# Matmuls without readers at two places of PE's queue in an attention, expert and dense-layer kernel

## The chip, the cores and the metric

The kernel runs on one core of a Trainium2 chip. The metric is device microseconds of one execution; a figure is the median of several. One further execution was taken by the hardware profiler, and all rows and durations below are from that one.

## What is computed

```python
attn_out = _attn_ref(q, k, v, f)                    # 4 x 8 heads, 576 x 64, causal, with decay
x = attn_out.transpose(0, 2, 1, 3).reshape(2304, 512)
# experts: each of 2304 tokens goes to the expert with the largest logit
logits = xn @ en.T / tau
expert_idx = np.argmax(logits, axis=1)
for e in range(8):
    mask = expert_idx == e
    h = np.maximum(x[mask] @ w1[e], 0.0)            # 512 -> 1024
    out[mask] = gate_w[mask, None] * (h @ w2[e])    # 1024 -> 512
# dense layers
h = x @ w_in                                        # 512 -> 2048
g = np.maximum(h, 0.0) + np.log1p(np.exp(-np.abs(h)))
y = g @ w_out                                       # 2048 -> 512
```

## The kernel before

Every instruction stands in the order in which the code writes it; each engine (PE, DVE, ACT, POOL) and SP, which issues most DMAs, works through its own queue in that order and waits for counters that the others raise.

**Attention** goes over 16 pairs of heads. Its last steps (`finish2`, `pick`) give every token's expert as a one-hot `oh`.

**Routing** turns these into slots of 128 tokens. `ranks` counts, on PE, each token's place in its expert's list into the PSUM tile `rk`; `places` (line 653) reads it with some ten small DVE steps; `route` (line 674) works out which expert each slot has, builds the 0/1 matrices `pm` (line 709) and the right side `rhs` (lines 772 to 774), and sums 20 matmuls into `pid` (line 778). From `pid` DVE makes `gidx`, by which POOL gathers the token rows `xg` from HBM (line 899). All of this has PE idle but for `ranks` and `pid`. Both PSUM tiles come from the attention's pool `ps_s`, tag `s`, three buffers.

**Experts** run in 13 phases written out in `phases`: a big one has two slots, a small one has one. A phase transposes its gathered rows (`xprep`: PE line 915, ACT line 916, DVE line 917), multiplies by `w1` (lines 983, 946), takes the relu, and multiplies by `w2` (line 933). Weights arrive by `wsplit` for the next phase: SP loads a 512 KB `raw` (lines 863, 866, 878), ACT rounds it to `wh` (line 887), DVE subtracts to get `wl` (line 888), which frees the `raw` for SP's next load; there are four `raw` buffers. Results go to `yd` in HBM by POOL's scatter (line 924).

After the last phase there may be more small slots than the plan foresaw. `tails` handles these under nested `tc.If` (line 1031): every engine reads the number of slots (line 1073) and branches. With these inputs no tail is run. A branch that isn't taken still leads each engine over an instruction that first waits until the engine's own earlier work is done and then raises the engine's counter by what the skipped code would have raised it. Whoever waits for work that stands behind the branch, or for memory that the skipped code would have used, waits for this instruction too.

**Dense layers** (`ffn`). SP first loads four tiles `y` from `yd` (line 1161), then more `raw` weights (line 1101). DVE, ACT and POOL convert the weights (`conv.step`, lines 1115 to 1121); when 16 of the 32 pieces are done, DVE scales the four `y` (line 1171), PE transposes them (line 1175), and from there PE runs `h` (line 1188) and `o` (line 1230) in turn to the end, while the rest of the weights is converted beside them.

Of the kernel before, what the change touches and what calls it, by code (L numbers as in the profile page):

```python
# [9 lines left out]
F32 = mybir.dt.float32  # L10
# [33 lines left out]
def body(ctx, tc, q, k, v, f, emb, tau, w1, w2, win, wout, out):  # L44
# [27 lines left out]
    with ExitStack() as acc:  # L72
        ps_s = attention(tc, g, acc, q, k, v, f, emb, tau, w1)
        ring = ctx.enter_context(tc.tile_pool(name="ring", bufs=16, reuse_waits="tile"))

        def wtile(dt=F32R):
            return (ring.tile([128, 1024], dt, name="wh", tag="wh"), ring.tile([128, 1024], dt, name="wl", tag="wl"))

        g.wtile = wtile
        with ExitStack() as rtx:  # L80
            route(tc, g, rtx.enter_context(tc.tile_pool(name="r_p", bufs=1)), ps_s)
    experts(tc, g, w1, w2, win, wout, out)


# [4 lines left out]
def attention(tc, g, acc, q, k, v, f, emb, tau, w1):  # L89
    nc = tc.nc  # L90
    ident, xd, ncum, nrm = g.ident, g.xd, g.ncum, g.nrm
    with ExitStack() as ctx:
        cst = ctx.enter_context(tc.tile_pool(name="a_cst", bufs=1))
# [4 lines left out]
        ps_s = acc.enter_context(tc.tile_pool(name="a_ps", bufs=3, space=PSUM))  # L98
# [353 lines left out]
        oh = cst.tile([128, T, E], BF16, name="oh")  # L452
# [64 lines left out]
        for n in range(n_all + Lg + 1):  # L517
# [47 lines left out]
                    g.pre.append(r)  # L565
            if n == n_all:
                rk = rank_start(tc, g, ps_s, oh)
        places(tc, g, cst, rk, oh)
    return ps_s


# [62 lines left out]
def rank_start(tc, g, psp, oh):  # L634
    nc = tc.nc
    rk = psp.tile([128, T + 1, E], F32, name="rk", tag="s")
    nc.tensor.matmul(rk, g.onesb, g.e4096, start=True, stop=False)
    nc.tensor.matmul(rk[:, T], g.onesb, oh[:, 0], start=False, stop=False)
    nc.tensor.matmul(rk[:, 1:T], g.onesb, oh[:, 0:1].to_broadcast([128, T - 1, E]), start=False, stop=False)
    ranks(nc, g, rk, oh, 0, T - 5)  # L640
    return rk


def ranks(nc, g, rk, oh, t0, t1):
    nc.tensor.matmul(rk[:, t0:t1], g.trib, oh[:, t0:t1], start=False, stop=False)
    for t in range(max(t0, 1), t1):
        nc.tensor.matmul(rk[:, t + 1:T + 1], g.onesb, oh[:, t:t + 1].to_broadcast([128, T - t, E]), start=False,
                         stop=(t == T - 1))

def places(tc, g, p, rk, oh):
    V = tc.nc.vector
    ranks(tc.nc, g, rk, oh, T - 5, T)
    sel = p.tile([128, T, E], F32, name="sel")
    V.tensor_tensor(sel, rk[:, 0:T], oh, op=ALU.mult)
    q = p.tile([128, T], F32, name="q")
    V.tensor_reduce(q, sel, op=ALU.add, axis=AX.X)
    g.n = g.const.tile([128, 3, E], I32, name="n")
    V.tensor_scalar(g.n[:, 0], rk[:, T], 0.0, None, op0=ALU.max)  # L660
    qi = p.tile([128, T], I32, name="qi")
    V.tensor_tensor(qi, q, g.inv.rearrange("p b r -> p (b r)"), op=ALU.add)
    V.tensor_scalar(g.n[:, 1], g.n[:, 0], 7, None, op0=ALU.logical_shift_right)
    li = p.tile([128, T], I32, name="li")
    V.tensor_scalar(li, qi, 127, None, op0=ALU.bitwise_and)
    V.tensor_scalar(g.n[:, 2], g.n[:, 1], 0x7FFFFFFE, None, op0=ALU.bitwise_and)
    g.lo = g.const.tile([128, T], F32, name="lo")
    V.tensor_copy(g.lo, li)
    g.code = g.const.tile([128, T, 1], I32, name="code")
    V.tensor_scalar(g.code[:, :, 0], qi, 7, None, op0=ALU.logical_shift_right)  # L670


def route(tc, g, p, psp):
    nc, lo, n, code = tc.nc, g.lo, g.n, g.code
# [4 lines left out]
    def tl(shape, nm, dt=F32):  # L679
        return p.tile(shape, dt, name=nm)  # L680
# [4 lines left out]
    start = tl([128, T, NSLOT], "start", BF16)  # L685
# [90 lines left out]
    pid = psp.tile([128, 3, NSLOT], F32, name="pid", tag="s")  # L776
    for t in range(T):
        nc.tensor.matmul(pid, pms[t], rhs[:, :, t], start=(t == 0), stop=(t == T - 1))
    pv = tl([128, 3, NSLOT], "pv")
    V.tensor_copy(pv[:, 1:3], pid[:, 1:3])  # L780
    V.scalar_tensor_tensor(g.gidx, pv[:, 1], 64.0, pv[:, 2], op0=ALU.mult, op1=ALU.add)
# [23 lines left out]
def gates(tc, g):  # L805
    nc = tc.nc
    V = nc.vector
    lt, nr, gs = g.lt, g.nr, g.gs
    nc.scalar.activation(nr[:, :, 0], g.nrm, ACTF.Sqrt)
    nc.scalar.preload_act_table_set(LN_EXP)  # L810
    V.tensor_scalar(nr, nr, 1e-6, None, op0=ALU.add)
    V.reciprocal(nr, nr)
    V.tensor_tensor(lt, lt, g.mx.to_broadcast([128, T, E]), op=ALU.subtract)
    V.tensor_tensor(lt, lt, nr.to_broadcast([128, T, E]), op=ALU.mult)
    nc.scalar.activation(lt, lt, ACTF.Exp)
    V.tensor_reduce(gs, lt, op=ALU.add, axis=AX.X)
    V.tensor_scalar(gs, gs, 1e-9, None, op0=ALU.add)
    V.reciprocal(gs, gs)
    for b in range(B):
        nc.gpsimd.dma_start(g.gd[b * S:b * S + 512, :].rearrange("(r p) o -> p (r o)", p=128), gs[:, 5 * b:5 * b + 4])  # L820
        nc.gpsimd.dma_start(g.gd[b * S + 512:b * S + S, :], gs[0:64, 5 * b + 4:5 * b + 5])
    nc.gpsimd.dma_start(g.gate, g.gd.rearrange("(t p) o -> p (t o)", p=128))


def experts(tc, g, w1, w2, win, wout, out):
    nc = tc.nc
# [10 lines left out]
    with ExitStack() as ctx:  # L837
        def pool(name, bufs, **kw):
            return ctx.enter_context(tc.tile_pool(name=name, bufs=bufs, reuse_waits="tile", **kw))
# [4 lines left out]
        ps_h = pool("e_ph", 3, space=PSUM)  # L844
# [219 lines left out]
        for ph in range(n_ph):  # L1064
            (big if phases[ph][0] == "b" else small)(ph)
            W.pop(ph)
            if ph == 0:
                gates(tc, g)
        while conv.done < PRE:
            conv.step(PRE - conv.done)  # L1070
        TW = [g.wtile() for _ in range(8)]
# [237 lines left out]
```

## Time and profile before

| | |
|---|---|
| median of 3 runs | 981.81 us (980.39 to 983.07) |
| the profiled execution | 986.43 us, of it 984.6 us from first to last instruction |
| mean granted clock of PE | 0.964 of full speed |
| PE busy | 904.0 us (92%) in 6340 matmuls |
| DVE, ACT, POOL busy | 647.8, 636.1, 362.0 us |
| routing, from the last `ranks` matmul to the first expert transpose | 252.13 to 267.33 us |
| from the last expert matmul to the first dense transpose | 546.66 to 564.97 us |

Times within the span count from its first instruction. The profiled execution is 4.6 us longer than the median of the unprofiled ones. A PE row's duration holds the fill and drain of the array, which overlap with the next one's; what a matmul costs in a stream is the distance between two starts.

### The profile page before, as it was taken

What the parts mean: (1) busy time and instruction counts of PE and PEld (TensorE: products, weight loads), DVE (VectorE), ACT (ScalarE), POOL (GpSimd) and SP (SyncE); (2) the same over time, 40 slices, a digit from 0 to 9 for tenths busy, and PEclk for the clock granted to TensorE, in tenths of its full rate; (3) what the DMA queues carried; (4) which work ended last, traced back from release to release, by engine and by line L of the source; (5) the groups of instructions that cost most, each with busy time, mean ns of one, the idle gap of its engine ahead of it and who ended that gap; (6) DMA issues with size and microseconds to landing.
All of it is one profiled execution on the core that took longest, in us unless ns stands there. A gap on an engine that the chain in (4) does not pass through costs nothing. (4 is left out here: it accounts for less than half of the span.)

```text
span 984.6 us, 17569 instructions
## 1 busy us (share of the span) xinstructions
PE 904.0 (92%) x6340; PEld 773.0 (79%) x6340; DVE 647.8 (66%) x1330; ACT 636.1 (65%) x1175; POOL 362.0 (37%) x438
## 2 busy tenths in 40 slices
PE   3999999999388899999998269999999999999998
PEld 2888888888276689889997258889988888998886
DVE  4888878887764668677674578885555545555454
ACT  4778877785463657666452257776767666677664
POOL 6655655551412321233222445652323222222221
PEclk9999999999589799999999789999999999999999
DMA  8766765840379889889874623301001001000001
GB/s 185 161 155 144 162 149 138 204 119 27 109 251 129 278 264 315 268 276 317 265 236 139 209 93 107 100 19 60 17 11 46 19 1 54 22 1 32 1 1 43
DMA packets 109852, 126.17 MB, mean 128 GB/s; under 512 B 62968, under 2 KB 72184, under 8 KB 109760
## 3 DMA queue, kind: packets, MB, share of 16 engines
q1 hardware_dynamic: 105952, 113.80, 41.7%
q0 software_dynamic: 3680, 11.03, 3.1%
q8 instruction: 52, 0.85, 0.4%
q14 instruction: 40, 0.33, 0.1%
q10 hardware_dynamic: 128, 0.16, 0.1%
HBM read 109.94 MB, written 15.03 MB: 127 GB/s over the span
## 5 line engine op out<-in xcount | busy, mean ns | idle before, releaser
L1218 DVE TENSOR_TENSOR gl<-e,gh 128x512 fp32r<-128x512 f32 (+1 forms) x80 | 97.6, 1220 | 152.7 <-ACT gh L1216 152.7
L1201 POOL TENSOR_TENSOR e<-u,e 128x512 f32<-128x512 f32 (+1 forms) x80 | 95.1, 1189 | 268.1 <-ACT u L1200 268.1
L888 DVE TENSOR_TENSOR wl<-raw,wh 128x1024 fp32r<-128x1024 f32 x100 | 122.8, 1239 | 72.4 <-ACT wh L887 69.9
L887 ACT ACTIVATE wh<-raw 128x1024 fp32r<-128x1024 f32 x100 | 104.7, 1057 | 50.4 <-DMA raw<-in_moe_w_dram 50.0
L1188 PE MATMUL h<-yth,wh 128*128 128x512 f32 (+1 forms) x320 | 120.0, 375 | 0.7 <-ACT yth L1176 0.7
L1188 PE MATMUL h<-ytl,wh 128*128 128x512 f32 (+1 forms) x320 | 118.5, 370 | 0.2 <-DVE ytl L1177 0.2
L1188 PE MATMUL h<-yth,wl 128*128 128x512 f32 (+1 forms) x320 | 118.4, 370 | 0.0
L1197 ACT ACTIVATE e<-h 128x512 f32<-128x512 f32 (+1 forms) x80 | 44.4, 555 | 107.2 <-PE h L1188 85.2
L1230 PE MATMUL o<-wl,gh 128*128 128x512 f32 x288 | 112.5, 391 | 0.0
L1230 PE MATMUL o<-wh,gh 128*128 128x512 f32 x288 | 112.4, 390 | 0.0
L1121 POOL TENSOR_TENSOR wl<-cv,wh 128x512 fp32r<-128x512 f32 x32 | 47.7, 1492 | 98.0 <-ACT wh L1120 79.0
L1230 PE MATMUL o<-wh,gl 128*128 128x512 f32 x288 | 80.8, 390 | 0.0
L300 ACT ACTIVATE pts<-pt 128x512 f16<-128x512 f32 (+3 forms) x128 | 58.7, 497 | 32.7 <-PE pt L313 17.6
L303 DVE SCALAR_TENSOR_TENSOR pts<-pt,pts 128x512 f16<-128x512 f32 (+3 forms) x128 | 69.7, 567 | 14.0 <-ACT pts L300 12.9
L946 PE MATMUL h<-xh,wh 128*128 128x256 f32 x256 | 73.2, 286 | 4.3 <-DVE hl L951 4.3
L946 PE MATMUL h<-xl,wh 128*128 128x256 f32 x256 | 73.0, 285 | 0.0
L946 PE MATMUL h<-xh,wl 128*128 128x256 f32 x256 | 73.0, 285 | 0.0
L933 PE MATMUL y<-wh,hh 128*128 128x512 f32 x168 | 69.2, 412 | 3.4 <-ACT hh L996 3.4
L1188 PEld LDWEIGHTS h<-yth,wh 128*128 128x128 f32 x320 | 60.6, 189 | 9.6 <-ACT yth L1176 1.1
L277 ACT ACTIVATE p<-sm,mx 128x512 f32<-128x512 f32 (+3 forms) x128 | 67.7, 558 | 0.0
L1188 PEld LDWEIGHTS h<-ytl,wh 128*128 128x128 f32 x320 | 60.6, 189 | 8.9 <-DVE ytl L1177 0.5
L933 PE MATMUL y<-wl,hh 128*128 128x512 f32 x168 | 67.1, 400 | 0.0
(273 smaller groups left out, 2424.7 us busy)
## 6 DMA issues: line engine op xcount, KB each, us to landing
raw<-in_moe_w_dram SPq DMA_DIRECT2D x104, 512.0 KB
cb<-ncum SPq DMA_DIRECT2D x32, 288.0 KB
raw<-in_moe_w_in_dram SPq DMA_DIRECT2D x16, 512.0 KB
raw<-in_moe_w_out_dram SPq DMA_DIRECT2D x16, 512.0 KB
cb<-ncum SPq DMA_DIRECT2D x32, 144.0 KB
out_dram<-ob SPq DMA_DIRECT2D x18, 256.0 KB
qt<-in_q_dram SPq DMA_DIRECT2D x32, 128.0 KB
kt<-in_k_dram SPq DMA_DIRECT2D x32, 128.0 KB
```

Source lines behind the costliest of these rows:

```text
L277: nc.scalar.activation(p[:, 0:n], s[:, 0:n], ACTF.Exp, scale=-1.0, bias=m)
L300: nc.scalar.activation(hi, ps, ACTF.Copy, scale=UP)
L303: nc.vector.scalar_tensor_tensor(lo, ps, UP, hi, op0=ALU.mult, op1=ALU.subtract)
L887: nc.scalar.activation(hi, r, ACTF.Copy)
L888: nc.vector.tensor_sub(lo, r, hi.bitcast(F32))
L933: nc.tensor.matmul(py[a], x[:, 128 * a:128 * a + 128], w[:, fb % 2], start=(fb == 0 and m == 0 and w is wh), stop=(fb == 7 and m == 1))
L946: nc.tensor.matmul(pl[:, a], w[:, fs], x[:, c], start=(c == 0 and m == 0), stop=(c == 3 and m == 2))
L1121: nc.gpsimd.tensor_sub(lo, a.bitcast(F32), hi.bitcast(F32))
L1188: nc.tensor.matmul(pl, w[:, fs], x[:, d], start=(d == 0 and m == 0), stop=(d == 3 and m == 2))
L1201: nc.gpsimd.tensor_sub(e, u, e)
L1218: nc.vector.tensor_sub(gl, d, gh.bitcast(F32))
L1230: nc.tensor.matmul(PO[c][a], x, w, start=(fb == 0 and m == 0 and w is wh), stop=(fb == FB - 1 and m == 1))
```

## The change

A matmul of `iof` (128 x 128, bf16, the numbers 0 to 127 in each row) with itself goes into a PSUM tile `idle` that nothing reads: 80 times behind the last of `ranks`, 40 times behind the last of `pid`, 220 times between the last expert phase and the branch of `tails`.

```diff
-        places(tc, g, cst, rk, oh)
+        places(tc, g, cst, rk, oh, ps_s)
...
+def busy(nc, g, psp, n):
+    t = psp.tile([128, 512], F32, name="idle", tag="s")
+    for _ in range(n):
+        nc.tensor.matmul(t[:, 0:128], g.iof, g.iof, start=True, stop=True)
...
-def places(tc, g, p, rk, oh):
+def places(tc, g, p, rk, oh, psp):
     V = tc.nc.vector
     ranks(tc.nc, g, rk, oh, T - 5, T)
+    busy(tc.nc, g, psp, 80)
     sel = p.tile([128, T, E], F32, name="sel")
...
         nc.tensor.matmul(pid, pms[t], rhs[:, :, t], start=(t == 0), stop=(t == T - 1))
+    busy(nc, g, psp, 40)
     pv = tl([128, 3, NSLOT], "pv")
...
             if ph == 0:
                 gates(tc, g)
+        t = ps_h.tile([128, 512], F32, name="idle", tag="h")
+        for _ in range(220):
+            nc.tensor.matmul(t[:, 0:128], g.iof, g.iof, start=True, stop=True)
         while conv.done < PRE:
             conv.step(PRE - conv.done)
```

The other engines' queues hold the same instructions in the same order as before. PE in the routing, with the change (`_49` ends the counters' names; `DMASW0` is the gather's; lines behind 655 are 8 or more higher than before):

```order
L647 MATMUL rk<-oh,onesb 128x8
L655 LDWEIGHTS iof
L655 MATMUL idle<-iof 128x128
...
L786 LDWEIGHTS pm [waits DVE_49,PE_49,Activation_49]
L786 MATMUL pid<-rhs,pm 128x75 [waits DVE_49]
...
L655 LDWEIGHTS iof
L655 MATMUL idle<-iof 128x128 [waits PE_49]
...
L924 MATMUL xt<-ident,xg 128x128 [waits DMASW0_49]
```

The 80 stand between `rk` and `pid`, the 40 between `pid` and the first transposes of gathered rows; each brings a load of its weights. They wait for no other engine.

PE at the branch, before:

```order
L933 MATMUL y<-wl,hh 128x512
L933 MATMUL y<-wh,hl 128x512
L1073 TENSOR_LOAD ids [waits Pool_49]
L1031 COMPARE_AND_BRANCH
...
L1031 UNCONDITIONAL_BRANCH [waits PE_49] x4
L1175 MATMUL yt<-ident,y_9160 128x128 [waits DVE_49,Activation_49]
```

and with the change:

```order
L942 MATMUL y<-wh,hl 128x512
L1080 LDWEIGHTS iof
L1080 MATMUL idle<-iof 128x128 [waits PE_49]
...
L1085 TENSOR_LOAD ids [waits Pool_49]
L1040 COMPARE_AND_BRANCH
...
L1040 UNCONDITIONAL_BRANCH [waits PE_49] x4
L1187 MATMUL yt<-ident,y_9503 128x128 [waits DVE_49,Activation_49]
```

The 220 stand ahead of the branch and of the instruction on the other path (shown with its wait for `PE_49`, PE's own counter) that PE must pass.

SP behind the branch, with the change (before, the same rows with the old line numbers):

```order
L1040 UNCONDITIONAL_BRANCH [waits SP_sequencer_49,DMAHW0_49,DMAHW1_49,DMAHW2_49,DMAHW3_49,DMAHW4_49,DMAHW5_49,DMAHW6_49,DMAHW7_49] x4
L1173 DMA y_9503<-yd 128x512 [waits DMASW4_49,DMASW3_49,DMASW5_49,DMASW2_49,DMASW6_49,DMASW1_49,DMASW7_49,DMASW0_49,DMAHW5_49,DVE_49,PE_49]
L1173 DMA y_9505<-yd 128x512 [waits DMAHW6_49,Activation_49]
L1173 DMA y_9507<-yd 128x512 [waits DMAHW7_49]
L1173 DMA y_9509<-yd 128x512 [waits DMAHW0_49]
L1113 DMA raw<-in_moe_w_in_dram 128x1024 [waits DMAHW1_49,DVE_49]
```

The first `y` load waits for PE's counter. In the built program of before it waits for 4592; PE's matmuls ahead of the branch bring the counter to 4364, and the instruction on the other path adds 240 once 4364 is reached. With the change the load waits for 4932; the matmuls, the 340 added ones among them, bring the counter to 4704, and the same instruction adds 240 once 4704 is reached.

## Rows read from the trace of the kernel before

**Rows 1.** The page's second part: busy tenths in 40 slices of 24.6 us.

```profile
PE   3999999999388899999998269999999999999998
PEclk9999999999589799999999789999999999999999
```

**Rows 2.** Timeline of PE, routing and first phase: start, duration, instructions, idle before and releaser.

```profile
251.84 0.29 PE L647 MATMUL rk<-oh,onesb 128*128 128x40 bf16 x5
261.28 1.43 PE L778 MATMUL pid<-rhs,pm 128*128 128x75 bf16 x20 [9.15 <-DVE rhs L774]
267.33 1.12 PE L915 MATMUL xt<-ident,xg 128*128 128x128 f32 x4 [4.62 <-DMA xg<-xd,gidx]
...
279.71 0.80 PE L933 MATMUL y<-wh,hh 128*128 128x512 f32 x1 [3.38 <-ACT hh L996]
```

**Rows 3.** Stretches of 4 us: PE, PEld, DVE, ACT, POOL busy, granted clock, DMA share, GB/s.

```profile
268.00:272.00 4.00, 3.90 (x11) 2.85 (x10) 2.96 (x4) 3.72 (x6) 3.17 (x4) 0.51 0.97 358
276.00:280.00 4.00, 0.62 (x3) 0.29 (x2) 0.79 (x1) 1.88 (x3) 0.00 (x0) 0.84 0.98 393
284.00:288.00 4.00, 4.00 (x20) 3.31 (x19) 2.65 (x4) 2.90 (x5) 0.00 (x0) 0.80 0.74 261
```

**Rows 4.** Timeline of PE from the last expert matmuls to the dense layers.

```profile
546.43 0.39 PE L933 MATMUL y<-wl,hh 128*128 128x512 f32 x1
546.66 0.39 PE L933 MATMUL y<-wh,hl 128*128 128x512 f32 x1
564.97 3.83 PE L1175 MATMUL yt<-ident,y 128*128 128x128 f32 x16 [17.93 <-DVE y L1171]
```

**Rows 5.** The chain that ended last, in order of time, 545 to 592 us.

```profile
553.82 0.33 SPq L1161
...
555.68 6.77 DMA raw<-in_moe_w_in_dram
```

**Rows 6.** Stretches of the dense layers' start, columns as in rows 3.

```profile
564.00:568.00 4.00, 3.03 (x14) 2.75 (x15) 4.00 (x7) 2.03 (x4) 1.57 (x1) 0.50 0.55 196
568.00:572.00 4.00, 3.09 (x13) 2.07 (x12) 3.37 (x6) 0.99 (x2) 0.00 (x0) 0.89 0.00 0
```

**Rows 7.** Timeline of PE: starts of 64- and 65-column matmuls, each with its own weights.

```profile
244.86 0.19 PE L375 MATMUL av<-vp,pts 128*128 128x65 f16 x1
244.89 0.19 PE L376 MATMUL av<-vp,pts 128*128 128x64 f16 x1
```

**Rows 8.** A 128-column bf16 weight load, by its line: columns as in rows 12.

```profile
L254 PEld LDWEIGHTS <-identb x128: 95/98/118, 19.4 to 237.2; 128*128 128x128 bf16 x128
```

**Rows 9.** Timeline of DVE, the last matrices for pid.

```profile
261.15 1.22 DVE L709 TENSOR_SCALAR pm<-iof,lo 128x128 bf16<-128x128 bf16 x7
```

**Rows 10.** Timeline of ACT in the first expert phase.

```profile
268.10 0.76 ACT L916 ACTIVATE xh<-xt 128x256 fp32r<-128x256 f32 x2 [12.47 <-PE xt L915]
...
278.12 1.06 ACT L887 ACTIVATE wh<-raw 128x1024 fp32r<-128x1024 f32 x1 [4.37 <-DMA raw<-in_moe_w_dram]
279.08 0.58 ACT L996 ACTIVATE hh<-ht 128x512 fp32r<-128x512 f32 x1
```

**Rows 11.** Timeline of PE: four transposes at either level of the clock.

```profile
584.96 1.12 PE L1175 MATMUL yt<-ident,yg 128*128 128x128 f32 x4 [6.52 <-POOL yg L1171]
...
603.89 0.60 PE L1175 MATMUL yt<-ident,yg 128*128 128x128 f32 x4
```

**Rows 12.** The branch's line on each queue: duration in ns (min/median/max), first and last start.

```profile
L1031 PEldq COMPARE_BRANCH  x1: 3745/3745/3745, 543.4 to 543.4; - x1
L1031 PEldq EVENT_SEMAPHORE  x1: 51/51/51, 547.2 to 547.2; - x1
L1031 POOLq INC_SWDGE_SEM  x1: 1220/1220/1220, 552.3 to 552.3; - x1
```

**Rows 13.** Timeline of SP behind the branch.

```profile
553.82 1.75 SPq L1161 DMA_DIRECT2D y<-yd  x4
555.68 3.24 SPq L1101 DMA_DIRECT2D raw<-in_moe_w_in_dram  x3
```

## The prediction

> **What bounds the kernel now.** The page's slices come first: PE is busy nine tenths nearly everywhere, and its clock is below full in two dips, slices 10 to 13 and 22 to 23 [rows 1]. These are the routing with the first expert phase and the passage to the dense layers, and there PE's timeline says who ends each wait. In the routing PE waits 9.15 us for DVE's `rhs` before `pid`, then 4.62 us for the gather [rows 2]. By then the clock is low: 0.51 over 268 to 272 us [rows 3], so the first expert matmuls run at 1.2 GHz. It is high again by 276, falls in the 3.38 us wait for `hh`, and is low once more until about 285.6 (0.80 over 284 to 288 us: 0.4 of the lost half, or 1.6 us, is low) [rows 2, 3].
>
> The second dip: PE ends its last expert matmul at 547.05 and has nothing until 564.97 [rows 4]. The chain of waits tells what fills that time: SP's four `y` loads from 553.82, behind them a `raw` load that is issued at 555.68 and lands 6.77 us later, DVE's conversion of it and the scaling of `y`, then the 16 transposes [rows 4, 5]. These begin at the low clock and end it: 0.50 over 564 to 568 us, 0.89 over the next four, so low until about 568.9 [rows 6]. PE is not what this passage waits for: SP is, and what holds SP. From there on PE is the chain, nearly without a gap, to the end.
>
> **The change, part by part.** It removes and moves nothing; it adds 340 pairs of weight load and matmul on PE.
>
> *The price of one pair.* 512 columns take 0.23 us at the high clock (starts 546.43 and 546.66 [rows 4]), 65 columns of 16-bit numbers, with a weight load of their own, 0.03 us [rows 7]. Both give 0.45 to 0.46 ns a column, so 128 columns cost 0.058 us; at the low level twice the array time, 0.107 us (128 columns at 1.2 GHz). The weight load lasts 98 ns by itself [rows 8], but since pairs with such loads follow each other every 0.03 us, loads run beside matmuls, and I count none. The Trainium skill's page "TensorE: Matmul & The Clock Gate" (section "Back-to-back issue gap") speaks against that: it gives about 81 ns for a sustained pair of 128 columns; by it the 220 below would take 17.8 us rather than 12.8. The rows 0.03 us apart disagree with a cost of the load, but they have 65 columns, so it is a rival below.
>
> *The 80 behind `ranks`.* They start at 252.13 (251.84 + 0.29 [rows 2]) at the low clock. All at that level they last 8.6 us, to 260.7; if the clock rises after 3.9 us, as it did at 564.97, 36 run at 0.107 and 44 at 0.058, 6.5 us, to 258.6. Even at twice 0.058 all the way they would end at 261.4; `pid` starts at 261.28. I cost them at nothing, covered by the 9.15 us wait for `rhs`; were they longer, `pid` would be late by the excess, here 0.2 us at most.
>
> *`pid` at a higher clock.* Its 20 matmuls take 1.43 us, but the last seven `pm` are only made until 262.37 (261.15 + 1.22 [rows 9]) and `pid` ends at 262.71. So at most 0.3 us can be saved; I take 0.1.
>
> *The 40 behind `pid`.* 2.3 us at the high clock, 4.3 at the low, from 262.7: done by 265.0 to 267.0, before the gather's 267.33 [rows 2]. No cost.
>
> *The first phase at a higher clock.* ACT's `xh` starts 0.77 us after the first transpose [rows 2, 10]. A set of four takes 1.12 us low and 0.60 high [rows 11]; half of that difference for the pair, 0.26 us. The 24 matmuls of `h` gain more, but PE then waits for `hh`, which stands in ACT's queue behind a `wh` that waits for a `raw` until 278.12 [rows 10]; that load is issued after ACT's first `wh` of the phase, so it can come earlier only by what `xh` does. The faster `h` becomes a longer wait, and the clock falls in it as before. Sum of this place: 0.36 us gained if the clock is held, nothing or a loss of 0.2 if not; I take -0.3.
>
> *The 220 before the branch.* They follow at 546.89 (546.66 + 0.23) and last 220 x 0.058 = 12.8 us, to 559.65. Nothing of PE's own is due before 564.97. But PE passes its branch only behind them: today its compare ends as the last matmul does, and the instruction that adds the 240 stands at 547.2, 0.15 us behind the matmul's end [rows 4, 12]. SP's first `y` load waits for that addition (4932 is over 4704). Today it is met 6 us early and POOL's own such instruction, which ends at 553.52, releases SP 0.3 us later [rows 12, 13]. With the change PE's addition comes at 559.65 + 0.16 (drain) + 0.15 = 559.96, and SP's load at 560.26 instead of 553.82: **6.4 us later**. SP issues in order, so the three `raw` behind it are late by as much, and with them DVE's conversion, the scaling, the transposes: PE gets its first dense work at about 571.4. Bounds: 0.055 us a pair gives 5.8 us, 0.062 gives 7.3.
>
> *The loads, when they come.* Today the three `raw` are issued over 3.24 us, since two of them wait for a buffer [rows 13]; DVE will have freed these by 560, so they follow at once and share the DMA engines with the `y`. The first, which the chain needs, may land later than 6.77 us after its issue. Below: no change; above: its 512 KB among 0.5 MB more than now, at the 358 GB/s of a full stretch [rows 3] 1.5 us; I take 0.4, nearer the lower end, since the stretch moves the same bytes.
>
> *The clock in the dense layers.* The 220 keep it high until 559.8, and then PE idles 11.6 us, against 17.9 today, at whose end it was low [rows 6]. I count no gain: the transposes start low again.
>
> Sum: -0.3 + 6.4 + 0.4 = **+6.5 us**. On the profiled execution that is 986.43 to 992.9; it was 4.6 us over the median of the runs, so against the median I forecast 981.81 + 6.5 = **988.3 us**. What a measurement of this kernel can tell from no change is about 0.3%, 2.9 us.
>
> **The rivals.** *(1) A pair costs more than its columns*, because its weight load doesn't quite hide. Between 0.058 and the bare load's 0.098 us, say 0.08: the 220 take 17.6 us, SP's load comes at 546.89 + 17.6 + 0.6 = 565.1, 11.3 us late, with the other terms 993.2 us. For it: both operands are the same tile. Against it: the 0.03 us between pairs [rows 7]. By the Trainium skill's 81 ns (same page) it would be 993.4, an estimate.
>
> *(2) SP's load isn't held*, so that the passage goes as it does now. That would be if the number it waits for were reached without PE's addition, or the addition didn't wait for the 220. Then only the clock acts. If it falls in the wait for `hh` and before 564.97, what is left is the -0.3: 981.5 us, no difference. If instead the high clock lasts through both, the result is **faster**: the first phase from 279.71 to 285.6 is low today, and 12 matmuls of 512 columns would take 0.23 instead of twice that, 2.8 us; the transposes before the dense layers are bound by DVE's scaling, and would save some 0.6 us; with 0.4 in the routing 3.8 us, 978.0 us. The point from which this decides is whether SP's first `y` load is issued before the 220 end. For it: PE has nothing else to do in these waits, and the low stretches are in the trace [rows 3, 6]. Against it: the order of SP's rows with its wait for `PE_49`, the two numbers, and the 3.38 us in which the clock fell with no such matmuls near.
>
> *(3) The change does nothing*, being hidden on an idle engine at both places: the same time as in the first half of (2), and counted there.
>
> **How the numbers follow.** The hold is in the program and not a matter of degree, and 12.8 us of matmuls cannot shrink below 220 x 128 columns at 2.4 GHz, 11.7 us, still 5 us past SP's 553.82. Forecast 0.83; (1) 0.06; (2) 0.11, of which 0.07 no difference and 0.04 faster. The forecast's own ends: 5.8 + 0 - 0.4 = +5.4 and 7.3 + 1.5 + 0.2 = +9.0; where the clock happens to rise after each wait moves a run by another 0.5 us or so (the runs shown spread over 2.7 us). That makes 985.0 to 992.0 us after cutting the upper end a little, since its three terms won't all be at their bound; what lies outside is (1), (2) and tails of the forecast, together under 0.2. Slower by over 0.3%: 0.83 + 0.06 = 0.89; within: 0.07; faster: 0.04.
>
> **What would show it.** Right: PE's timeline has the 220 from about 546.9 to 559.7, some 0.058 us apart; PE's queue passes the branch line just behind; SP's four `y` are issued near 560, released by that and no longer by POOL; the first dense transpose is near 571, at 0.5 of the clock; from there the rows repeat today's. The routing has `pid` and the first transposes at the times of today within half a microsecond, with the clock high in 268 to 272. Wrong: SP's `y` load near 554 with the 220 still running (2); starts 0.08 us apart (1); or `pid` later than 261.3, which would mean that the 80 are not covered.

## The result, and the profile after

| | before | after |
|---|---|---|
| median of 5 runs, us | 981.81 (980.39 to 983.34) | 988.92 (987.34 to 990.82) |
| ratio, 95% interval | | 1.0075 (1.005 to 1.010) |
| the profiled execution, us | 986.43 | 987.34, of it 985.6 from first to last instruction |
| mean granted clock of PE | 0.964 | 0.977 |
| from the last expert matmul's start to the first dense transpose, us | 18.31 | 26.65 |

The change costs 7.1 us of the median, with an interval from about 5 to 10; forecast were 6.5. The clock is higher on the mean, and the kernel is slower.

The two profiled executions differ by less, 0.9 us, than the medians (the prediction had 992.9 us for the one of after). The experts took 294.8 us in the one of before, from the last row of `ranks` (251.84) to the last expert matmul's (546.66), and 287.4 us in the one of after (252.19 to 539.57). In the profiles of the ten experiments that stretch lies between 286.9 and 292.2 us, the longest without pairs in the routing (292.2) and with them (290.5) not far apart, so one pair of traces can't show a gain there. A part of the difference lies far behind the routing: over 336 to 340 us PE's clock is 0.50 in the one of before and 1.00 in the one of after. Times below are therefore counted from the last expert matmul, and totals come from the timed runs.

The passage first. These are three instructions of the branch line in the profile of after (engine's queue, operation, count: ns least/median/most, first to last start in us; PEldq is PE's sequencer):

```profile
L1040 POOLq INC_SWDGE_SEM  x1: 1220/1220/1220, 544.1 to 544.1; - x1
L1040 PEldq COMPARE_BRANCH  x1: 3362/3362/3362, 551.7 to 551.7; - x1
L1040 PEldq EVENT_SEMAPHORE  x1: 51/51/51, 555.1 to 555.1; - x1
```

Then, each in a block of its own, PE's timeline of after around it, the added pairs by their line, SP's timeline, and one piece of the chain of waits (start, duration, what):

```profile
539.57 0.39 PE L942 MATMUL y<-wh,hl 128*128 128x512 f32 x1
...
566.22 3.68 PE L1187 MATMUL yt<-ident,y 128*128 128x128 f32 x16 [13.96 <-DVE y L1183]
```

```profile
L1080 PE MATMUL idle<-iof x220: 218/219/230, 539.8 to 552.0; 128*128 128x128 bf16 x110
```

```profile
555.23 2.19 SPq L1173 DMA_DIRECT2D y<-yd  x4
557.51 1.32 SPq L1113 DMA_DIRECT2D raw<-in_moe_w_in_dram  x3
```

```profile
557.51 6.18 DMA raw<-in_moe_w_in_dram
```

The 220 start from 539.8 to 552.0, 12.2 / 219 = 0.056 us apart (forecast 0.058). PE reaches its compare at 551.7, as the pairs end; the compare takes 3.36 us, and PE's addition stands at 555.1. SP's first `y` load follows at 555.23, 15.66 us behind the last expert matmul's start; before it was 553.82 - 546.66 = 7.16 [rows 4, 13]. POOL's instruction, which released SP before [rows 12], is over at 545.3, 10 us too early to matter now. From `y` to the first transpose it is 10.99 us, before 11.15. So the passage is what the prediction said, held by PE, but by 8.5 us in this trace and not 6.4.

In the routing, PE's timeline of after:

```profile
252.19 0.29 PE L647 MATMUL rk<-oh,onesb 128*128 128x40 bf16 x5
252.34 6.16 PE L655 MATMUL idle<-iof 128*128 128x128 bf16 x80
261.38 1.39 PE L786 MATMUL pid<-rhs,pm 128*128 128x75 bf16 x20 [2.88 <-DVE rhs L782]
262.57 3.95 PE L655 MATMUL idle<-iof 128*128 128x128 bf16 x40
267.13 0.66 PE L924 MATMUL xt<-ident,xg 128*128 128x128 f32 x4 [0.61 <-DMA xg<-xd,gidx]
...
278.08 0.50 PE L942 MATMUL y<-wh,hh 128*128 128x512 f32 x1 [2.38 <-ACT hh L1005]
```

And the windows (start:end, length, busy time and instructions of PE, PEld, DVE, ACT, POOL, then the granted clock, the DMA share and GB/s):

```profile
268.00:272.00 4.00, 3.91 (x17) 3.16 (x18) 3.46 (x5) 3.28 (x5) 3.23 (x4) 1.00 0.98 355
276.00:280.00 4.00, 1.28 (x3) 0.80 (x4) 2.43 (x3) 3.08 (x4) 0.00 (x0) 0.94 0.99 345
280.00:284.00 4.00, 4.00 (x15) 3.20 (x14) 2.45 (x4) 2.61 (x3) 0.00 (x0) 0.64 0.84 272
284.00:288.00 4.00, 4.00 (x26) 3.52 (x25) 3.85 (x5) 3.46 (x5) 0.00 (x0) 1.00 0.75 227
...
564.00:568.00 4.00, 1.78 (x9) 1.81 (x10) 3.93 (x7) 1.23 (x2) 1.57 (x1) 0.50 0.71 246
568.00:572.00 4.00, 3.09 (x13) 2.11 (x12) 3.61 (x7) 1.79 (x3) 0.00 (x0) 0.80 0.16 61
```

One window of the kernel before, which rows 3 leave out:

```profile
280.00:284.00 4.00, 3.85 (x11) 2.63 (x12) 3.30 (x4) 2.04 (x3) 0.00 (x0) 0.50 0.65 163
```

The 80 and the 40 are covered: `pid` comes 9.19 us behind the start of the last `ranks` (before 9.44). It starts at 261.38, past the 261.3 that the prediction named as a sign of being wrong, only because the last `ranks` start 0.35 us later in this trace. The clock is full over 268 to 272 us, where it was 0.51 [rows 3]. It still falls in the wait for `hh`, but PE runs low for less long: 0.64 over 280 to 284, 1.00 over the next four, where before it was 0.50 from 280 and 0.80 in the next. The dense transposes start low, as forecast, 0.50 over 564 to 568.

### The profile page after: what moved, and what is told of

It is laid out like the page before. It is cut to its first block, busy times and chain, and to the rows that moved or that the text cites. A ratio compares the mean times of both kernels' runs of the same rounds, so it can differ in the third digit from the quotient of the medians.

```text
span 985.6 us, 18250 instructions
## 1 busy us (share of the span) xinstructions
PE 920.2 (93%) x6680; PEld 790.6 (80%) x6680; DVE 647.7 (66%) x1330; ACT 636.1 (65%) x1175; POOL 365.9 (37%) x438
## 5 line engine op out<-in xcount | busy, mean ns | idle before, releaser
L1200 PEld LDWEIGHTS h<-yth,wl 128*128 128x128 f32 x320 | 60.4, 189 | 7.8
```

What stands on the lines that cost most here:

```text
L1200: nc.tensor.matmul(pl, w[:, fs], x[:, d], start=(d == 0 and m == 0), stop=(d == 3 and m == 2))
```

## The experiments

Each kernel was timed in five rounds, beside the kernel before on the same chip. A ratio is of its time to that of the kernel before, with the 95% interval in brackets; a difference in us is worked out from the ratio and the median of the kernel before (981.39, 981.41 or 980.82 us).

### Each part alone

The routing alone leaves out the 220; its reverse leaves out `busy(..., 80)` and `busy(..., 40)`.

```diff
-        t = ps_h.tile([128, 512], F32, name="idle", tag="h")
-        for _ in range(220):
-            nc.tensor.matmul(t[:, 0:128], g.iof, g.iof, start=True, stop=True)
```

> The 80 and the 40 pairs in the routing alone. Theory A (the 220 hold SP's y load, the routing hardly matters): 0 to 0.5 us faster than before, 981.3 to 981.8 us. Rival R (the routing's pairs are worth more, since in the profile with the change the first expert phase's y matmuls start at 278.08 instead of 279.71): 1.5 to 2.5 us faster, 979.3 to 980.3 us. If the pairs cost something there, slower than 982.3 us.

> The 220 pairs before the branch alone. Theory A (the y load comes 0.45 us plus SP's 0.3 us after the last pair): 6.4 us later than before in the passage, 988.2 us. Theory A2 (PE's compare at the branch takes its 3.4 us only after the pairs, where it lay under the last expert matmuls before, so that the y load comes some 3.2 us after the last pair): 9 to 10 us later, 991 us. If the 220 cost nothing, 981.8 us.

The routing alone: 978.57 us against 981.39, ratio 0.9972 (0.9955 to 0.999), **-2.7 us**. The 220 alone: 989.66, ratio 1.0073 (1.0047 to 1.0098), **+7.2 us**. So the whole loss is that of the 220, and the routing is a real gain, several times the forecast's 0.3. The routing's gain is of the size of rival R (1.5 to 2.5), and theory A's (0 to 0.5) lies outside its interval. For the 220 alone the times don't decide between theories A and A2, as the interval of +4.6 to +9.6 holds both; the traces below do. These are three lines of the profile with the 220 alone:

```profile
L1038 PEldq COMPARE_BRANCH  x1: 2130/2130/2130, 550.9 to 550.9; - x1
L1038 PEldq EVENT_SEMAPHORE  x1: 51/51/51, 553.1 to 553.1; - x1
553.21 2.92 SPq L1171 DMA_DIRECT2D y<-yd  x4
```

The first `y` load is at 553.21, 14.40 us behind the last expert matmul's start at 538.81: 7.24 later than before, near the time lost. The first dense transpose comes 8.25 us later, since SP takes 2.92 us to issue the four `y` where it took 1.75 [rows 13].

### How long PE's addition holds SP

The number of pairs before the branch was changed, with nothing in the routing:

```diff
-        for _ in range(220):
+        for _ in range(100):
```

> 100 pairs before the branch instead of 220, none in the routing; they end 5.6 us after the last expert matmul. Theory A: the y load would be free at 6.3 us after it, when POOL's instruction releases it anyway: within 0.5 us of before, 981.8 us. Theory A2: free at 5.6 + 3.2 = 8.8 us after it, against some 6.3: 2.5 to 3 us slower, 984.5 us.

The other kernel has `range(300)`.

> 300 pairs before the branch, none in the routing. If SP's y load is held by PE's addition, which comes a few us of the compare's own behind the last pair: 80 pairs more than in the run with 220 are 80 x 0.0557 = 4.5 us later, so +7.2 + 4.5 = +11.7 us, 993.1 us; in the trace the y load comes about 19 us behind the start of the last expert matmul, within 0.5 us of PE's addition. If the hold saturates, because something else then ends the passage: about +7 us, 988.6. If the compare's own time lies fully under the longer row of pairs (the drain alone behind the last pair): E + 0.2 + 16.7 + 0.3, y load 17.2 us behind the last expert matmul's start, +9 to +10 us, 991 us.

100 pairs: 983.31 us, ratio 1.0017 (1.0 to 1.0034), +1.7 us. 300 pairs: 992.23 against 980.82, ratio 1.012 (1.01 to 1.0139), +11.8 us, as expected of a hold that grows with the pairs. The time of the 100 lies between the two theories, and its interval (0 to +3.3) reaches both. The branch line in the two and SP's first loads, 100 first:

```profile
L1038 POOLq INC_SWDGE_SEM  x1: 1220/1220/1220, 542.9 to 542.9; - x1
L1038 PEldq COMPARE_BRANCH  x1: 3896/3896/3896, 543.8 to 543.8; - x1
L1038 PEldq EVENT_SEMAPHORE  x1: 51/51/51, 547.7 to 547.7; - x1
547.82 2.41 SPq L1171 DMA_DIRECT2D y<-yd  x4
```

```profile
L1038 PEldq COMPARE_BRANCH  x1: 3852/3852/3852, 554.7 to 554.7; - x1
L1038 PEldq EVENT_SEMAPHORE  x1: 51/51/51, 558.6 to 558.6; - x1
558.68 2.77 SPq L1171 DMA_DIRECT2D y<-yd  x4
```

With 100, the last pair starts at 544.1 and so ends by about 544.3. Had the addition come just behind it, POOL's instruction (over at 544.1) and PE would have been done together, and SP would have been released some 6 us behind the last expert matmul, no later than before. It was released at 547.82, behind PE's 547.7, since the compare lasts 3.90 us by itself: theory A2. The traces side by side, times in us from the start of the last expert matmul (its own start in brackets):

| pairs before the branch | last pair starts | compare starts, lasts | PE's addition | first `y` load | first dense transpose | time against before |
|---|---|---|---|---|---|---|
| none, kernel before (546.66) | | -3.3, 3.75 | 0.5 | 7.16 | 18.31 | |
| none, routing alone (538.28) | | -3.3, 4.09 | 0.9 | 6.94 | 17.59 | -2.7 |
| 100 (538.36) | 5.7 | 5.4, 3.90 | 9.3 | 9.46 | 19.43 | +1.7 |
| 220 (538.81) | 12.5 | 12.1, 2.13 | 14.3 | 14.40 | 26.56 | +7.2 |
| 220, the change (539.57) | 12.4 | 12.1, 3.36 | 15.5 | 15.66 | 26.65 | +7.4 |
| 300 (538.10) | 16.9 | 16.6, 3.85 | 20.5 | 20.58 | 30.79 | +11.8 |

In the two kernels without pairs PE's sequencer comes to its compare 3.3 us ahead of the last expert matmul, and most of the compare's 3.7 to 4.1 us lies under matmuls that were issued already. With pairs it comes there only 0.3 to 0.4 us ahead of the last pair, and 1.8 to 3.6 us of the compare stand bare, between the last pair's start and the addition. From 100 pairs to 300, whose compares last alike, the first `y` load moves by 11.1 us, 0.056 us a pair, which is what a pair takes; the time rises by 10.1 us, 0.050 a pair, with an interval of some 2.5 us.

### The same 220 behind the branch

```diff
         ...
+        t = ps_h.tile([128, 512], F32, name="idle", tag="h")
+        for _ in range(220):
+            nc.tensor.matmul(t[:, 0:128], g.iof, g.iof, start=True, stop=True)
         units = [(c, fb) for c in range(NC) for fb in range(FB)]
```

> The same 220 pairs, none in the routing, but behind the branch: in ffn ahead of its first transposes. PE passes the branch as in the kernel before. Theories A and A2 alike: the y load is issued some 6.5 us after the last expert matmul as before, no loss; the clock is high later into the wait, 0 to 1 us faster, 980.8 to 981.8 us. A rival in which the pairs themselves cost (reads, the clock's budget, the queue): slower by the same 6 to 9 us as in front of the branch, 988 us or more.

981.86 us, ratio 0.9997 (0.9974 to 1.0019). The same pairs, in the same idle time, cost nothing (-2.6 to +1.9 us) where no addition stands behind them: it is the place that costs, not the work. PE's timeline and windows of this kernel:

```profile
544.66 12.44 PE L1248 MATMUL idle<-iof 128*128 128x128 bf16 x220 [0.89 <-ACTq L1038]
561.62 3.83 PE L1182 MATMUL yt<-ident,y 128*128 128x128 f32 x16 [4.51 <-DVE y L1178]
```

```profile
556.00:560.00 4.00, 1.10 (x20) 0.93 (x17) 1.11 (x3) 1.02 (x2) 2.48 (x2) 0.99 0.98 345
560.00:564.00 4.00, 2.38 (x12) 2.42 (x12) 3.97 (x7) 1.64 (x3) 1.57 (x1) 0.50 0.77 271
564.00:568.00 4.00, 3.31 (x10) 1.96 (x10) 3.43 (x7) 1.38 (x3) 0.00 (x0) 0.50 0.06 24
568.00:572.00 4.00, 4.00 (x15) 3.17 (x14) 0.58 (x1) 0.74 (x2) 0.00 (x0) 0.72 0.59 175
```

They gain nothing either. They end 4.51 us too early, the clock is down to 0.50 when the transposes start, and it stays low through 568 and beyond, longer than in the kernel before (on this below).

### The routing's two places one by one

> Of the routing's pairs only the 80 behind the ranks; nothing before the branch. With both the routing gained 2.7 us (1.0 to 4.4). If the first phase's clock makes it, the 80 alone gain little, since they end before pid and some 8 us before the phase's first matmuls: 0 to 1 us faster, 981 us. If the gain has nothing to do with the clock there, as much as with both: 978.7 us.

> Of the routing's pairs only the 40 behind pid. They start at the low clock, last 4.3 us and end just before the gather lands; the clock can rise in them or in the transposes behind. If the first phase's clock makes the gain: nearly all of it, 979 to 980 us. My prediction's term for the routing would give 981.1 to 981.8 us.

Only the 80: 979.48 us, ratio 0.9979 (0.9961 to 0.9997). Only the 40: 979.38, 0.9972 (0.9956 to 0.9988). Each alone gives about what both give, -2.1 and -2.7, so which of them does it isn't told apart; the interval of the 80 (-0.3 to -3.8) holds both of its expectations. A window of each at the first phase's start, the 80 first:

```profile
268.00:272.00 4.00, 4.00 (x11) 3.13 (x11) 3.48 (x5) 3.71 (x4) 3.39 (x3) 0.52 0.90 301
```

```profile
268.00:272.00 4.00, 4.00 (x18) 3.05 (x18) 3.54 (x5) 3.32 (x5) 3.29 (x3) 1.00 0.99 328
```

With the 40 alone the clock is full there, with the 80 alone it is as low as before (0.51 [rows 3]), and the times are alike. This speaks against the simple reading, that the gain comes from the clock at the first phase's start.

Over all twelve profiles, it takes 35.0 to 37.8 us from the last row of `ranks` to the first matmul of the second phase (the first `h` of 256 columns) with nothing in the routing, but for one of 34.0, mean 36.5 (six profiles), and 35.1 to 35.7 with pairs there, but for one of 33.2, mean 35.0 (six). That would put about 1.5 us of the gain in the first phase, but single profiles overlap, and nothing of it is seen any more at the last expert matmul: from the last row of `ranks` to there the medians of the two groups are 287.8 and 287.7 us. That the pairs in the routing gain is shown by the times; where the gain arises, and whether by the clock, stays open.

### A better place in the dense layers, and all together

PE waits 6.5 us for POOL's `yg` before the second set of dense transposes, which start low [rows 11]. 100 pairs were put ahead of these:

```diff
                     if fb == 2 + 3 * a:
+                        if c == 0 and a == 0:
+                            t = ps_t.tile([128, 512], F32, name="idle", tag="T")
+                            for _ in range(100):
+                                nc.tensor.matmul(t[:, 0:128], g.iof, g.iof, start=True, stop=True)
                         next(turn, None)
```

> 100 pairs in another place alone: in the dense layers behind the first three h, where PE idles 6.5 us for POOL's yg and then runs four transposes and some ten h matmuls at the low clock, with PE on the chain from there on. They last 5.6 us and fit in. If a high clock is worth what the rows at either level say: 1.12 - 0.60 for the transposes and about 1.6 for the h, 2.1 us faster, 979.7 us. If the pairs delay PE or the clock falls all the same: 981.4 us or more.

979.48 us, ratio 0.9979 (0.996 to 0.9998), -2.1 as expected. PE's timeline and a window of this kernel:

```profile
570.80 5.76 PE L1283 MATMUL idle<-iof 128*128 128x128 bf16 x100
577.51 0.66 PE L1182 MATMUL yt<-ident,yg 128*128 128x128 f32 x4 [0.95 <-POOL yg L1178]
```

```profile
576.00:580.00 4.00, 3.05 (x23) 2.53 (x21) 3.93 (x5) 2.45 (x5) 2.74 (x3) 1.00 0.22 89
```

The set takes 0.66 us where it took 1.12 [rows 11], and the `h` matmuls behind it run at the full clock. In this profile the first `h` of the dense layers, which stand ahead of the pairs, ran low, as they did not in the kernel before (on this below).

The next kernel has the 80 and 40, these 100, and 290 behind the branch, so as to last until the first transposes:

> The routing's 80 and 40 as in the change; 290 pairs behind the branch (16.2 us, where 220 left PE idle for 4.5 us and the clock fell in it) instead of 220 before it; and the 100 in the dense layers' gap. Theory A2 (only the place before the branch costs): 2.7 + 2.1 + 0.6 for the transposes at the high clock, 976 us, faster than both kernels. If many such matmuls cost something of their own, no faster than the routing's alone, 978.7 us; if the 290 outlast the wait for y, up to 1 us is lost again.

978.03 us, ratio 0.9971 (0.9955 to 0.9988): -2.8, not the sum. PE's timeline of it:

```profile
540.79 16.35 PE L1250 MATMUL idle<-iof 128*128 128x128 bf16 x290 [0.88 <-ACTq L1040]
557.58 1.50 PE L1184 MATMUL yt<-ident,y 128*128 128x128 f32 x12 [0.43 <-DVE y L1180]
560.29 0.66 PE L1184 MATMUL yt<-ident,y 128*128 128x128 f32 x4 [1.21 <-DVE ytl L1186]
561.64 0.50 PE L1197 MATMUL h<-yth,wh 128*128 128x512 f32 x1 [0.69 <-ACT yth L1185]
562.36 0.80 PE L1197 MATMUL h<-ytl,wh 128*128 128x512 f32 x1 [0.22 <-DVE ytl L1186]
562.96 0.63 PE L1197 MATMUL h<-yth,wl 128*128 128x512 f32 x1
```

The 290 last to 0.43 us before the transposes, and these run at the full clock, in 1.50 us for twelve. But they wait on DVE and ACT among themselves, and then the clock falls: `h` matmuls of 512 columns take 0.63 us instead of 0.39 until about 565.5. In the kernel before these `h` run at the full clock, so it looks as if the 290 had moved the low time from the transposes, which wait for DVE anyway, onto work that PE itself sets. The next kernel leaves the 290 out:

> The 80 and 40 in the routing and 100 ahead of the second set of transposes in the dense layers; nothing between the last expert matmul and the transposes. If the two gains are of different stretches and add up (-2.7 of the routing alone, -2.1 of the 100 alone): 976.6 us, ratio 0.995. If a gain in the routing is taken up again by what follows it, or if the two singly were high by chance: 978 to 979 us, as the run with three places (978.03), ratio 0.9965 to 0.9975. If the 290 behind the branch cost that run something: below 977.5.

977.79 us against 980.82, ratio 0.9966 (0.9943 to 0.9989), -3.3. The interval holds the sum (-4.8) and no addition at all (-2.7); whether the two gains add isn't told apart. This kernel and the one with three places are faster than before and than the change; they are not told apart from the routing alone.

The same matmuls in the kernel before, and then in this last one:

```profile
570.54 0.39 PE L1188 MATMUL h<-yth,wl 128*128 128x512 f32 x1
```

```profile
557.43 3.83 PE L1184 MATMUL yt<-ident,y 128*128 128x128 f32 x16 [17.63 <-DVE y L1180]
561.95 0.79 PE L1197 MATMUL h<-yth,wh 128*128 128x512 f32 x1 [0.69 <-ACT yth L1185]
563.27 0.63 PE L1197 MATMUL h<-yth,wl 128*128 128x512 f32 x1
```

Without the 290 the first `h` run low as well, so the 290 need not be what made them low. Seven or eight of these first `h` take 0.63 us or more in four of the twelve profiles: with the 220 behind the branch, with the 100 alone, with the 290, and in this last kernel. In the other eight none does. With the 100 alone and in the last kernel nothing was added between the last expert matmul and these `h`; the pairs come only behind them. The four are the kernels with pairs behind the branch; what makes their first `h` low, or whether it is chance, no run here shows.

## Why the prediction was right, and where not

- **SP's `y` load is held by PE's addition.** Right. It comes 0.1 us behind that addition in every kernel with pairs before the branch, and moving the pairs behind the branch takes the loss away. Rivals (2) and (3), not held or nothing done, fall.
- **The price of a pair.** Right: 0.056 us against 0.058. Rival (1), 0.08 us, falls, and with it, for this pair, the 81 ns of the Trainium skill's page "TensorE: Matmul & The Clock Gate" (section "Back-to-back issue gap").
- **When PE's addition comes.** This step failed. The prediction had it "559.65 + 0.16 (drain) + 0.15", having read from rows 12 that the compare "ends as the last matmul does", and so as lasting until the matmuls are done. That the two ended together was a coincidence: in the eight kernels with no pairs before the branch the compare ends 0.5 to 1.3 us behind the last expert matmul's start. It takes 2.1 to 4.5 us by itself, began early, and was hidden by matmuls already issued. With the pairs ahead of it it starts late. The hold was forecast as 6.4 us; it is 7.2 in the profile of the 220 alone and 8.5 in that of the change. The pairs are 0.5 us shorter than forecast and SP's own step 0.2; the compare adds 1.5 and 2.8, where the prediction had it at nothing.
- **The loads.** The three `raw` are issued over 1.32 us, where it was 3.24, as the prediction said. The first lands 6.18 us after its issue, not later than before (6.77), so the 0.4 us for sharing the DMA engines isn't seen. Instead SP takes longer to issue the four `y`, 2.19 us in the change and 2.92 with the 220 alone, before 1.75.
- **The dense clock.** Right: the transposes start at 0.50 after 13.96 us of waiting.
- **The routing.** The term of -0.3 was too small; it measured -2.7 (-1.0 to -4.4). The prediction took the high clock to be lost whole in the wait for `hh`. In the profile of the change it is lost there, but PE is low for a shorter time behind it: 0.64 over 280 to 284 and 1.00 after, where before 0.50 and 0.80. The first `y` matmul comes at 25.89 us from the last `ranks` (before 27.87), though this alone varies from 24.5 to 27.9 without pairs. What the term lacked stays open.
- **The dips.** Slice 13 of rows 1 isn't in the routing or the first phase, as the prediction has it: it spans 320 to 344 us, in later expert phases, where PE's clock is 0.61 over 320 to 324 and 0.50 over 336 to 340.

That the total came within 1 us is in part luck. The routing's gain was put 2.4 us too low and the compare at nothing, two errors of opposite sign. Taken alone, the two places make -2.7 + 7.2 = +4.5 us, and the change +7.4 (4.9 to 9.8); with the intervals of all three these aren't told apart.

## What to carry to other kernels

Filler work on an idle engine is free only if nothing that others wait for stands behind it in that engine's queue; a branch counts, since the additions of the path not taken wait in order like everything else. Behind the branch the same pairs cost nothing here, but they gained nothing either, also where they lasted nearly to the end of the wait. The 100 before the second set of transposes, behind which PE's own work follows at once, gained 2.1 us. And an instruction that ends together with its neighbour need not be waiting for it: its duration may be its own, and bare once the cover is moved.

## What the runs showed of the hardware

PE's compare at this branch lasts 2.13 to 4.49 us in the twelve profiles, that of DVE, SP, ACT and POOL 0.05 to 0.07. While the change's compare runs (551.7 to 555.1), the DMA engines are all but idle; the instruction queue moves 2 packets of 0.03 MB in 549 to 557 us, one of them at 552.8, within the compare. This is the queue's row in the view of the DMAs:

```profile
q8 instruction: 2, 0.03, 1.4%
```

In eleven of the twelve profiles such a packet comes 1.0 to 1.8 us after the compare's start. In that of the 220 alone it comes 0.3 us before it, and there the compare is the shortest, 2.13 us. So the compare ends 2.3 to 2.9 us behind a packet in all twelve, whenever it started.

That would fit a fetch of the code behind the branch. The Trainium skill's page "Runtime: NRT & Kernel Launch" (section "Instruction fetch mechanics") says that a taken branch to code outside of what was fetched ahead waits for a DMA of it. The packets agree with it, but no run here took the fetch away, so the cause stays open.
